# Attention, MoE and routed experts in one kernel: weight loads paced, output weights converted one step later, one chunk's routing moved to TensorE

## The chip, the cores and the metric

One core of a Trainium2 chip runs the whole program. The metric is device microseconds of one execution on that core, lower is better. A measurement of this kernel can tell about 0.2% from no change.

## What is computed

Three stages follow each other, all in float32 for 2304 tokens: windowed attention with 8 heads, a gated product of two projections, and eight experts of which each token uses one.

```python
def _attn_ref(q, k, v):               # q, k, v: (4, 8, 576, 64)
    scores = scale * np.matmul(q, k.transpose(0, 1, 3, 2))
    mask = (rel >= 0) & (rel < 128)
    scores = np.where(mask, scores + bias[None], -1000000000.0)
    scores = scores - np.max(scores, axis=-1, keepdims=True)
    attn = np.exp(scores)
    attn = attn / (np.sum(attn, axis=-1, keepdims=True) + 1e-09)
    return np.matmul(attn, v)

def _moe_ref(x, w_a, w_b, w_out):     # float64 weights, 512 x 1536 and 1536 x 512
    return ((x @ w_a) * (x @ w_b)) @ w_out

def _moe2_ref(x, modality_id, w_gate, modality_bias, w1, w2):
    logits = x @ w_gate + modality_bias[modality_id]
    e_idx = np.argmax(logits, axis=1)
    ...
    for e in range(E):
        h = np.maximum(x[mask] @ w1[e], 0.0)
        out[mask] = gate_w[mask, None] * (h @ w2[e])
```

## The kernel before

The tokens are cut into 18 tiles of 128 and these into seven chunks of 3, 2, 2, 3, 3, 3 and 2 tiles. For each chunk c the program takes 12 steps j, one for each block of 128 columns of the inner width 1536. A step multiplies the chunk by block j of both projections (`mm_ab`, L502: 24 matmuls, since weight and data are each split into a rounded part and a remainder), multiplies the two results (`gf`), and adds the previous step's result times a block of the output weights to the accumulators (`mm_out`, L515 in chunk 0, L519 later). Between these, each step advances the attention of the next chunk's tiles: `score_mm` (L254, L258), select and maximum (L266, L272), exponential (L282), sum and reciprocal (L288, L290), norm (L301), transposes (`pt_tr`, L310), mask selection on GpSimd (L326, L328), product with the values (`a_pv`, L378) and its evacuation (`pv_out`, L387).

The weights arrive as float64. In chunk 0 they are converted as the steps go. For a weight pair (block j of both projections, 1 MB, `wab_load`, L435) VectorE builds float32 words in three operations (`f64_ops`: `one`, L422, and two `more`, L426; the tile is `f64f`), ScalarE casts the rounded part (`hi`, L449) and VectorE subtracts for the remainder (`rest`, L452). `wab_jobs` returns these five jobs in that order. An output weight (512 KB, `wo_load`, L464) needs three operations (`wo_jobs`, tile `f64o`); it is used in that form in chunk 0 and stored (`wo_f`, L475) for the later chunks. The raw and the converted output weights share four buffers. `step00` is step 0 of chunk 0 and `step0` every other step of it.

TensorE, ScalarE and VectorE run in the order in which the program is written; SP's queue, which issues nearly all transfers in order, is ordered by the scheduler. In `step0` the list `da` holds the remainder of pair j + 1 and the three word operations of pair j + 2, the list `db` the two operations on the softmax sums and the three of the output weight, and they are taken in turns.

The routing of a finished chunk (logits, argmax, place in the expert's list) has two forms, chosen by `RD`. A chunk in `RD` gets dot products on VectorE: `rd_step` runs one expert a step, one operation per tile (`junk`, L601), with the expert's gate row broadcast by a 256 KB load (`wgt`, L596). Any other chunk gets `route`: four transposes (L531), a copy, eight small matmuls (L539) and the rank chain (`route_fin`), one tile after another in `step`. Before the change chunk 0 uses `route` and chunks 1 to 5 use dot products; the dot products of chunk c run in the steps of chunk c + 1.

Of the kernel before, what the change touches and what calls it, by code (L numbers as in the profile page):

```python
# [16 lines left out]
P = 128  # L17
# [4 lines left out]
def attn_moe_moe2(ctx: ExitStack, tc, q, k, v, moe_w_a, moe_w_b, moe_w_out, modality_id,  # L22
# [15 lines left out]
    SK = 3  # L38
    CAP = 0
    QD = 1  # L40
    RD = (1, 2, 3, 4, 5)
    PCB = 1
    LDA = 6
    SAT = 3
# [235 lines left out]
    def score_exp(it):  # L280
        for h in range(2):
            nc.scalar.activation(out=it.p[:, h, :], in_=it.p[:, h, :], func=AF.Exp, bias=it.mx[:, 2 + h:3 + h],  # L282
                                 scale=-1.0, accum_out=it.mx[:, 4 + h:5 + h])
# [177 lines left out]

    def wo_load(j):
        r = m1.tile([P, DM, 2], U32, tag="wo", bufs=WOB, name="wor")
        nc.sync.dma_start(out=r.rearrange("p a b -> p (a b)"), in_=moe_w_out.bitcast(U32)[j * P:(j + 1) * P, :])  # L464
        wraw["o", j] = r

    def wo_jobs(j):
# [509 lines left out]
    def step00():  # L977

        n, p1 = CH[0] * P, pairs[1, 0]
        w1, w2, wo = job.pop(1)[3:], wab_jobs(2), wo_jobs(0)  # L980
        job[2] = w2
        i0 = live[n0] = score_mm(p1, 0)
        mm_ab(0, 0, 0, (3,))
        i1 = live[n0 + 1] = score_mm(p1, 1)
        mm_ab(0, 0, 1, (3,))
        w1[0]()
        score_red(i0)
        w1[1]()
        asb = m1.tile([P, MT * P], F32, tag="asb", bufs=1, name="asb")
        nc.scalar.copy(out=asb[:, :n], in_=ab_ps[0][:, :n])  # L990
        gf = m1.tile([P, MT * P], F32, tag="g", bufs=2, name="gf")
        nc.vector.tensor_tensor(out=gf[:, :n], in0=ab_ps[1][:, :n], in1=asb[:, :n], op=ALU.mult)
        score_exp(i0)
        score_inv(i0)
        score_red(i1)
        prep_va(p1)
        score_nrm(i0)
        mm_ab(0, 1, 0)
        wo[0]()
        pt_tr(i0)  # L1000
        pt_cp(i0)
        prep_vd(p1)
        score_exp(i1)
        w2[0]()
        score_inv(i1)
        score_nrm(i1)
        for f in (wo[1], w2[1], wo[2], w2[2], w2[3]):
            f()
        new_preps(goal[2], goal[0])
        cur["s"] = goal[0]  # L1010
        return (0, 0, gf), [n0 + 1], [n0]

    def step0(j, pend, sc, tp):
# [4 lines left out]
        if j + 2 < NJ:  # L1018
            job[j + 2] = wab_jobs(j + 2)
        js = job.get(j + 2, [])  # L1020

        da = [job.pop(j + 1)[4]] if j + 1 in job else []
        da += js[:3]
        di = [f for g in sc for f in score_invs(live[g])]
        dw = wo_jobs(j)
        db = di[:1] + dw[:1] + di[1:] + dw[1:]
        while da or db:
            for d in (da, db) if j > 1 else (db, da):
                if d:
                    d.pop(0)()  # L1030
        psa = mm_ab(0, j, 0) if j > 1 else ab_ps[0]
        asb = m1.tile([P, MT * P], F32, tag="asb", bufs=1, name="asb")
        nc.scalar.copy(out=asb[:, :n], in_=psa[:, :n])
# [14 lines left out]
        for g in new:  # L1048
            c_, hp_, t_ = items[g]
            live[g] = score_mm(pairs[c_, hp_], t_)  # L1050
        for f in js[3:4]:
            f()
        for g in new:
            score_red(live[g])
        for g in new:
            score_exp(live[g])
        new_preps(goal[j + 2], goal[j])
        mm_out(*pend, wo_t[j - 1])
        if last:
# [8 lines left out]
    def step(c, j, pend, sc, tp):  # L1068
# [23 lines left out]
        for r in ranks:  # L1092
            if r[0] < 2:
                next(r[1])
                r[0] += 1
        if c > 2:
            rd_step(j)
        new_preps(goal[k + 2], goal[k])
        if c == 1 and j + 2 < NJ:
            wo_fetch(j + 2, c)  # L1100
# [28 lines left out]
            x_split(c + 1, range(1, KD))  # L1129
        for g in new:  # L1130
            score_exp(live[g])
        if c == 2:
            rd_step(j)
        if pend is not None:
            mm_out(*pend)
        if tr and tr[0][0] in (0, 2, 4):
# [59 lines left out]
    for c in range(NC):  # L1196
        n = CH[c] * P
        for j in range(NJ):
            if c == 0:
                if j == 0:  # L1200
                    pe.enter_context(tc.manual_schedule(engines={
                        mybir.EngineType.PE, mybir.EngineType.Activation, mybir.EngineType.DVE}))
                if j + 4 < NJ:
                    wab_load(j + 4)
                if j + 1 < NJ:
                    wo_load(j + 1)
                if j == CJ:
                    with tc.issue_after(mark["pt"]):
                        consts_b()
# [307 lines left out]
```

## Time and profile before

| what | value |
|---|---|
| median of 3 runs | 838.18 us (838.05 to 838.37) |
| profiled execution | 838.99 us, span 837.2 us |
| mean granted TensorE clock | 0.989 |
| TensorE matmuls busy | 803.4 us (96%) |
| weight loads busy | 721.1 us (86%) |
| VectorE / ScalarE / GpSimd busy | 563.1 / 460.0 / 237.4 us |
| data moved | 147.23 MB, mean 176 GB/s |

Busy shares are averages over stages that differ: a stage's own limit is read from its windows and from what each idle stretch waited for. A row's idle time stands in brackets with the engine and line that released it.

### The profile page before, as it was taken

To read this page: it belongs to the slowest core of one execution; us is meant where nothing else is said; L and a number is where in the kernel's file an instruction comes from. 1 tells how busy PE (TensorE), PEld (TensorE's weight loads), DVE (VectorE), ACT (ScalarE), POOL (GpSimd) and SP (SyncE) were. 2 spreads that over 40 slices of the span, in tenths; PEclk is the share of its full clock that TensorE was granted. 3 is DMA by queue.
4 is the path that set the end of the run, shared out by engine and by line. 5 is a ranking of instruction groups with operands and counts; after the bars stand their busy time and mean duration, and the time that the engine had idled before them with its cause. 6 is when DMAs were issued, how large, how long until landed. Compare 5 with 4: busy or idle time off the path is not lost.

```text
span 837.2 us, 14381 instructions
## 1 busy us (share of the span) xinstructions
PE 803.4 (96%) x4662; PEld 721.1 (86%) x4662; DVE 563.1 (67%) x1603; ACT 460.0 (55%) x1159; POOL 237.4 (28%) x365
## 2 busy tenths in 40 slices
PE   9969999999998999999999999999999999999994
PEld 7856777999887899999999999999888998979893
DVE  7778997777788776667877776468575544447420
ACT  7844555877766766666666644233345443547410
POOL 5312242343344332232222331120133030115101
PEclk9998999999999999999999999999999999999997
DMA  8993336676666795554555544557428554649301
GB/s 240 377 391 104 115 111 191 198 229 218 194 185 191 197 211 161 151 152 136 161 153 155 129 142 123 147 165 241 169 83 306 193 193 134 168 135 303 117 25 40
DMA packets 79781, 147.23 MB, mean 176 GB/s; under 512 B 14223, under 2 KB 42031, under 8 KB 79696
## 3 DMA queue, kind: packets, MB, share of 16 engines
q1 hardware_dynamic: 76144, 136.48, 54.1%
q0 software_dynamic: 3552, 9.73, 3.2%
q8 instruction: 39, 0.64, 0.3%
q14 instruction: 46, 0.38, 0.2%
HBM read 120.25 MB, written 22.12 MB: 170 GB/s over the span
## 4 chain that ended last, share of the span: by engine, by line
PE 63%; DVE 12%; issue 8%; DMA 8%; ACT 5%; POOL 2%; SPq 1%; POOLq 0%; ACTq 0%; DVEq 0%
PE ps_ab L502 26%; PE acc L519 10%; PE ps_h L1270 8%; PE ps_y L1253 7%; PE acc L515 3%; DVE junk L601 3%; PE ps_o L378 2%; DMA wraw<-in_moe_w_b 2%; PE ps_s L258 2%; PE ps_p L310 1%; DMA wraw<-in_moe_w_a 1%; DMA wo_f<-f64o 1%; DMA kk<-in_k 1%; DMA tab<-tinit 1%; DVE p L272 1%
## 5 line engine op out<-in xcount | busy, mean ns | idle before, releaser
L502 PE MATMUL ps_ab<-xr,wab 128*128 128x384 f32 (+1 forms) x2016 | 326.2, 316 | 1.9 <-DVE gf L1167 1.0
L502 PEld LDWEIGHTS ps_ab<-xr,wab 128*128 128x128 f32 x2016 | 307.3, 188 | 14.0 <-issue 4.4
L519 PE MATMUL acc<-wo,g 128*128 128x512 f32 x540 | 135.1, 393 | 0.0
L326 POOL TENSOR_SCALAR_AFFINE_SELECT pt<-pc 128x512 fp32r<-128x512 f32 (+1 forms) x72 | 46.3, 643 | 269.3 <-DVE pc L324 244.2
L519 PEld LDWEIGHTS acc<-wo,g 128*128 128x128 f32 x540 | 96.9, 188 | 16.9
L1270 PE MATMUL ps_h<-xT,w1s 128*128 128x384 f32 x576 | 104.3, 337 | 0.0
L1253 PE MATMUL ps_y<-w2s,h 128*128 128x512 f32 x432 | 104.0, 394 | 0.0
L1270 PEld LDWEIGHTS ps_h<-xT,w1s 128*128 128x128 f32 x576 | 99.7, 188 | 1.3 <-issue 0.5
L1253 PEld LDWEIGHTS ps_y<-w2s,h 128*128 128x128 f32 x432 | 79.8, 188 | 15.7
L601 DVE CUSTOM_DVE_ANT_0 junk<-x,wgt 128x512 f32<-128x512 f32 x104 | 77.4, 744 | 2.9 <-DMA wgt<-in_wgt 0.6
L282 ACT ACTIVATE p<-p,mx 128x128 f32<-128x128 f32 x144 | 56.8, 396 | 31.0 <-DVE mx L272 30.7
L301 ACT ACTIVATE p<-p,mx 128x128 f32<-128x128 f32 x120 | 41.7, 395 | 38.8 <-DVE mx L290 38.6
L387 ACT COPY u<-ps_o 64x384 f32<-64x384 f32 x120 | 56.9, 474 | 7.6 <-PE ps_o L378 6.2
L1105 ACT CAST g<-gf 128x384 fp32r<-128x384 f32 (+1 forms) x60 | 28.2, 470 | 50.6 <-DVE gf L1103 50.2
L1106 DVE TENSOR_TENSOR g<-gf,g 128x384 fp32r<-128x384 f32 (+1 forms) x60 | 30.3, 505 | 37.8 <-ACT g L1105 37.3
L886 DVE TENSOR_TENSOR w2s<-wr,w2s 128x1024 fp32r<-128x1024 f32 x24 | 29.4, 1225 | 38.0 <-ACT w2s L885 37.9
L1260 POOL DMA_INDIRECT out<-y,idx x18 | 21.2, 1176 | 114.7 <-ACT y L1259 113.2
L1103 DVE TENSOR_TENSOR gf<-ps_ab,asb 128x384 f32<-128x384 f32 (+1 forms) x60 | 30.1, 502 | 29.6 <-PE ps_ab L502 22.6
L1273 ACT ACTIVATE h<-ps_h 128x384 fp32r<-128x384 f32 x48 | 23.6, 492 | 44.0 <-PE ps_h L1270 44.0
L886 DVE TENSOR_TENSOR w1s<-wr,w1s 128x1024 fp32r<-128x1024 f32 x28 | 34.3, 1224 | 16.7 <-ACT w1s L885 16.7
L392 POOL TENSOR_TENSOR xf<-u 128x128 f32<-128x128 f32 x60 | 33.9, 564 | 39.5 <-ACT u L387 39.5
L328 POOL TENSOR_SCALAR_AFFINE_SELECT pt<-pc 128x512 fp32r<-128x512 f32 (+1 forms) x72 | 45.0, 625 | 0.0
(218 smaller groups left out, 1207.5 us busy)
## 6 DMA issues: line engine op xcount, KB each, us to landing
wo<-wo_d SPq DMA_DIRECT2D x60, 512.0 KB, 4.2
wr<-in_moe_w SPq DMA_DIRECT2D x56, 512.0 KB, 4.8
wgt<-in_wgt SPq DMA_DIRECT2D x40, 256.0 KB, 3.6
wraw<-in_moe_w_a SPq DMA_DIRECT2D x12, 512.0 KB, 8.9
wraw<-in_moe_w_b SPq DMA_DIRECT2D x12, 512.0 KB, 8.6
wor<-in_moe_w_out SPq DMA_DIRECT2D x12, 512.0 KB, 3.9
wo_d<-wo SPq DMA_DIRECT2D x12, 512.0 KB, 3.1
kr<-in_k SPq DMA_DIRECT2D x24, 256.0 KB, 4.3
```

Of the source, the lines that this page charges most:

```text
L282: nc.scalar.activation(out=it.p[:, h, :], in_=it.p[:, h, :], func=AF.Exp, bias=it.mx[:, 2 + h:3 + h], scale=-1.0, accum_out=it.mx[:, 4 + h ...
L301: nc.scalar.activation(out=it.p[:, h, :], in_=it.p[:, h, :], func=AF.Copy, scale=it.mx[:, 6 + h:7 + h])
L326: nc.gpsimd.affine_select(out=it.pt[:, :, 0], in_=pc, pattern=pat + [[-1, P]], base=0, channel_multiplier=1, compare_op=ALU.is_gt, fill=0.0)
L328: mark["pt"] = nc.gpsimd.affine_select(out=it.pt[:, :, 1], in_=pc, pattern=pat + [[1, P]], base=0, channel_multiplier=-1, compare_op=ALU.i ...
L387: nc.scalar.copy(out=u[o:o + 64], in_=it.po[o:o + 64, 1 - h:4 - h])
L392: nc.gpsimd.tensor_tensor(out=xf, in0=u[:, 0], in1=u[:, 2], op=ALU.add)
L502: nc.tensor.matmul(ps[:, :n], lhsT=w[:, m, r, kk * P:(kk + 1) * P], rhs=xr[:, s, kk, :n], start=(idx == 0), stop=(idx == len(terms) - 1))
L519: nc.tensor.matmul(acc[c, t], lhsT=g[:, r, t * P:(t + 1) * P], rhs=w[:, s, :], start=(j == 0 and idx == 0), stop=(j == NJ - 1 and idx == 2))
L601: nc.vector.tensor_tensor_reduce(out=junk, in0=x2[:, 0:DM], in1=wgt[0][:, e % 2], scale=1.0, scalar=0.0, op0=ALU.mult, op1=ALU.add, accum_ ...
L886: nc.vector.tensor_tensor(out=dst[:, 1], in0=srcw, in1=dst[:, 0], op=ALU.subtract)
L1253: nc.tensor.matmul(pss[t], lhsT=h[:, r, f, t * P:(t + 1) * P], rhs=W2[f // 2][:, s_, f % 2, :], start=(f == 0 and i == 0), stop=(f == 7 an ...
L1270: nc.tensor.matmul(ps, lhsT=W1[f // 2][:, r, kk, (f % 2) * P:(f % 2 + 1) * P], rhs=xT[:, s_, kk, :], start=(kk == 0 and i == 0), stop=(kk ...
```

## The change

In chunk 0, from step 2 on, the output weight converted in step j is j - 1 (the last step does two), and it is loaded one step later. From step 1 to step 7 the load of weight pair j + 4 is put behind the latest output weight load in SP's queue. The turns of the two lists are written out, with the sums' and the output weight's operations ahead of the next pair's words. In step 0 the cast of pair 2 is left out and done in step 1 behind the new tile's score product; step 1's other weight work comes after its exponential. Chunk 1 leaves `RD`, so its routing is done by `route` in chunk 2.

```diff
-    RD = (1, 2, 3, 4, 5)
+    RD = (2, 3, 4, 5)
...
     def wo_load(j):
         r = m1.tile([P, DM, 2], U32, tag="wo", bufs=WOB, name="wor")
-        nc.sync.dma_start(out=r.rearrange("p a b -> p (a b)"), in_=moe_w_out.bitcast(U32)[j * P:(j + 1) * P, :])
+        mark["wo"] = nc.sync.dma_start(out=r.rearrange("p a b -> p (a b)"),
+                                       in_=moe_w_out.bitcast(U32)[j * P:(j + 1) * P, :]).ins
...
-        for f in (wo[1], w2[1], wo[2], w2[2], w2[3]):
+        for f in (wo[1], w2[1], wo[2], w2[2]):
             f()
...
-        da = [job.pop(j + 1)[4]] if j + 1 in job else []
+        w = job.pop(j + 1, None)
+
+        di = [f for g in sc for f in score_invs(live[g])]
+        dw = [f for i in ((j - 1, j) if last else (j - 1,)) if j > 1 for f in wo_jobs(i)]
+        da, db = [w[4]] if w else [], di[:1] + dw[:1] + di[1:] + dw[1:]
         da += js[:3]
-        di = [f for g in sc for f in score_invs(live[g])]
-        dw = wo_jobs(j)
-        db = di[:1] + dw[:1] + di[1:] + dw[1:]
-        while da or db:
-            for d in (da, db) if j > 1 else (db, da):
-                if d:
-                    d.pop(0)()
+        for d in () if j == 1 else (da, db, db, db, da, db, da, db, da, db, db, db):
+            if d:
+                d.pop(0)()
+        assert j == 1 or not da and not db
...
-        for f in js[3:4]:
-            f()
+        if j == 1:
+            w[3]()
+        else:
+            for f in js[3:4]:
+                f()
         for g in new:
             score_red(live[g])
         for g in new:
             score_exp(live[g])
+        if j == 1:
+            for f in da + js[3:4]:
+                f()
...
-        if c > 2:
-            rd_step(j)
+        rd_step(j)
...
-        if c == 2:
-            rd_step(j)
...
-                if j + 4 < NJ:
-                    wab_load(j + 4)
-                if j + 1 < NJ:
-                    wo_load(j + 1)
+                if j == 0:
+                    wab_load(4)
+                if j != 1:
+                    wo_load(max(j, 1))
+                if 0 < j < NJ - 4:
+                    with tc.issue_after(mark["wo"]):
+                        wab_load(j + 4)
```

Three places show how the instructions move. The first is chunk 0, steps 0 to 2. On ScalarE the cast of pair 2 (`wab_765`, now `wab_815`) stood between the norm of step 0 (L301) and the scaling of the next query pair (L232):

```order
 L282 ACTIVATE p,mx<-p,mx 128x128 x2
 L301 ACTIVATE p<-p,mx 128x128 x2
-L449 CAST wab_765<-f64f 128x2x512
 L232 ACTIVATE qq<-qr_1_671,qscale 64x256 x2
-L1033 COPY asb<-ps_ab_727 128x384
-L323 CAST pc<-ps_p 128x2x128
-L387 COPY u<-ps_o 64x384 x2
+L1034 COPY asb<-ps_ab_727 128x384
+L323 CAST pc<-ps_p 128x2x128
+L387 COPY u<-ps_o 64x384 x2
+L449 CAST wab_815<-f64f 128x2x512
```

It now follows the evacuation of step 1 (L387). On VectorE, in step 2, pair 3's remainder (`wab_829`), the sums (L288, L290), output weight 2 (`f64o`) and pair 4's words (`wraw_666`) stood like this:

```order
L452 TENSOR_TENSOR wab_829<-f64f,wab_829 128x2x512
L288 TENSOR_SCALAR mx<-mx 128x2
L422 TENSOR_SCALAR f64f<-wraw_666 128x1024
L422 TENSOR_SCALAR f64o<-wor 128x512
L426 SCALAR_TENSOR_TENSOR f64f<-wraw_666,f64f 128x1024
L290 RECIPROCAL mx<-mx 128x2
L426 SCALAR_TENSOR_TENSOR f64f<-wraw_666,f64f 128x1024
L426 SCALAR_TENSOR_TENSOR f64o<-wor,f64o 128x512 x2
```

And now, with pair 2's remainder (`wab_815`) and pair 3's words (`wraw_209`) just ahead, at the end of step 1, and output weight 1 in the place of 2:

```order
L452 TENSOR_TENSOR wab_815<-f64f,wab_815 128x2x512
L422 TENSOR_SCALAR f64f<-wraw_209 128x1024
L426 SCALAR_TENSOR_TENSOR f64f<-wraw_209,f64f 128x1024 x2
L452 TENSOR_TENSOR wab_829<-f64f,wab_829 128x2x512
L288 TENSOR_SCALAR mx<-mx 128x2
L422 TENSOR_SCALAR f64o<-wor 128x512
L290 RECIPROCAL mx<-mx 128x2
L422 TENSOR_SCALAR f64f<-wraw_666 128x1024
L426 SCALAR_TENSOR_TENSOR f64o<-wor,f64o 128x512
L426 SCALAR_TENSOR_TENSOR f64f<-wraw_666,f64f 128x1024
L426 SCALAR_TENSOR_TENSOR f64o<-wor,f64o 128x512
L426 SCALAR_TENSOR_TENSOR f64f<-wraw_666,f64f 128x1024
```

The reciprocal has moved ahead of pair 4's words, and the output weight's last operation ahead of the pair's.

The second place is SP's queue ahead of the values of the next head pair (`vr_1_673`). Before, the weight pairs stood there in a row up to the last; `wraw_1102` to `wraw_1272` are pairs 9 to 11, `wraw_846` and `wraw_945` pairs 6 and 7:

```order
L435 DMA wraw_1102<-in_moe_w_b 128x1024
L435 DMA wraw_1184<-in_moe_w_a 128x1024
L435 DMA wraw_1184<-in_moe_w_b 128x1024
L435 DMA wraw_1272<-in_moe_w_a 128x1024
L435 DMA wraw_1272<-in_moe_w_b 128x1024
L435 DMA wraw_846<-in_moe_w_a 128x1024
L435 DMA wraw_846<-in_moe_w_b 128x1024
L435 DMA wraw_945<-in_moe_w_a 128x1024
L435 DMA wraw_945<-in_moe_w_b 128x1024
L156 DMA qr_2_675<-in_q 128x256
L464 DMA wor<-in_moe_w_out 128x1024
L161 DMA vr_1_673<-in_v 128x3x128
```

Now, with `wraw_841` pair 6 and `wraw_940` pair 7:

```order
L464 DMA wor<-in_moe_w_out 128x1024
L435 DMA wraw_841<-in_moe_w_a 128x1024
L435 DMA wraw_841<-in_moe_w_b 128x1024
L161 DMA vr_1_673<-in_v 128x3x128
L156 DMA qr_3_679<-in_q 128x256
L476 DMA wo_f<-f64o 128x512
L390 DMA z<-u 64x128 x2
L464 DMA wor<-in_moe_w_out 128x1024
L435 DMA wraw_940<-in_moe_w_a 128x1024
L435 DMA wraw_940<-in_moe_w_b 128x1024
```

Of the pairs that stood ahead of the values only 5 and 6 are left there; pair 7 and the later ones each follow an output weight load. The store of output weight 0 (`wo_f`) is the one of its kind that comes first, before and now.

The third place is VectorE in chunk 2, between the maximum (L272) and the sums (L288) of one tile. Before, the two dot products (L601) stood there in each of eight steps:

```order
L272 ISA mx 128x1
L601 ISA junk,lgr<-x_2779,wgt 128x512
L601 ISA lgr 128x1
L601 ISA junk,lgr<-x_2782,wgt 128x512
L601 ISA lgr 128x1
L288 TENSOR_SCALAR mx<-mx 128x2
```

Now no L601 is left in this chunk. In two steps for each of the two tiles stand rows of the rank chain, here those of the second of these steps:

```order
L272 ISA mx 128x1
L559 TENSOR_SCALAR sc<-sc 128x1
L560 RECIPROCAL x_2776<-sc 128x1
L577 TENSOR_TENSOR osum<-osum,oh 128x8
L579 TENSOR_TENSOR ra<-ps_r,ereg 128x8
L580 TENSOR_TENSOR ra<-ra,oh 128x8
L581 TENSOR_REDUCE sc<-ra 128x1
L582 CAST po_all<-sc 128x1
L288 TENSOR_SCALAR mx<-mx 128x2
```

TensorE gets, once for each tile, four transposes (L532), eight small products (L540) and the two matmuls that give the rank (L575, L576).

## Rows read from the trace of the kernel before

**Rows 1.** Stage windows: us, busy us (count) of PE, PEld, DVE, ACT, POOL, PEclk.

```profile
36.70:71.03 34.33, 25.15 (x98) 18.75 (x98) 28.60 (x58) 15.99 (x44) 6.85 (x13) 0.85 0.86 321
...
78.47:134.08 55.61, 55.20 (x260) 43.91 (x259) 53.76 (x97) 26.79 (x64) 20.36 (x27) 1.00 0.44 130
...
144.09:212.50 68.41, 67.89 (x501) 62.98 (x499) 49.80 (x172) 55.04 (x154) 25.96 (x41) 1.00 0.68 214
212.50:289.80 77.30, 70.69 (x479) 62.27 (x479) 60.74 (x194) 52.72 (x152) 31.82 (x48) 1.00 0.66 183
```

**Rows 2.** Timeline of PE, 26 to 90 us: start, us, what, idle before.

```profile
50.74 2.07 PE L254 MATMUL ps_s<-kk,qq 128*128 128x256 f32 x4 [4.07 <-ACT qq L232]
...
64.63 0.76 PE L310 MATMUL ps_p<-ident,p 128*128 128x128 f32 x2 [4.08 <-ACT p L301]
...
66.89 4.70 PE L515 MATMUL acc<-f64o,gf 128*128 128x512 f32 x6
71.03 4.73 PE L502 MATMUL ps_ab<-xr,wab 128*128 128x384 f32 x24
...
76.29 2.74 PE L515 MATMUL acc<-f64o,gf 128*128 128x512 f32 x6
```

**Rows 3.** Windows after the second stop, and in chunk 2.

```profile
64.00:66.00 2.00, 1.37 (x4) 1.13 (x5) 1.97 (x5) 1.21 (x4) 0.00 (x0) 0.50 0.01 2
...
251.00:255.00 4.00, 2.94 (x17) 2.35 (x17) 3.36 (x11) 3.11 (x8) 0.72 (x2) 1.00 0.69 213
```

**Rows 4.** Timeline of ACT, 26 to 90 us.

```profile
49.23 1.04 ACT L449 CAST wab<-f64f 128x1024 fp32r<-128x1024 f32 x1 [3.03 <-DVE f64f L426]
...
61.68 0.51 ACT L197 CAST vv<-vr 128x384 fp32r<-128x384 f32 x1 [3.30 <-DMA vr<-in_v]
```

**Rows 5.** Timelines of DVE, 26 to 90 and 88 to 165 us.

```profile
62.45 0.43 DVE L422 TENSOR_SCALAR f64o<-wor 128x512 uint32<-128x512 uint32 x1 [2.54 <-DMA wo_f<-f64o]
...
86.39 1.22 DVE L452 TENSOR_TENSOR wab<-f64f,wab 128x1024 fp32r<-128x1024 f32 x1
...
92.78 0.55 DVE L1039 TENSOR_TENSOR gf<-ps_ab,asb 128x384 f32<-128x384 f32 x1
...
94.46 1.58 DVE L452 TENSOR_TENSOR wab<-f64f,wab 128x1024 fp32r<-128x1024 f32 x1
```

**Rows 6.** Timeline of SP's queue, 14 to 75 us.

```profile
39.05 0.33 SPq L435 DMA_DIRECT2D wraw<-in_moe_w_a  x1
...
53.05 0.38 SPq L161 DMA_DIRECT2D vr<-in_v  x1
```

**Rows 7.** Waits, 212.5 to 289.8 us: us, times, longest.

```profile
ACT p L301 <- DVE mx L290: 15.1, 11, 1.8
```

**Rows 8.** Lines of DVE by form, 212.5 to 289.8 us.

```profile
L601 DVE CUSTOM_DVE_ANT_0 junk<-x,wgt 128x512 f32<-128x512 f32 x16 | 15.0, 939 | 0.3
```

**Rows 9.** Tile f64f, 36 to 140 us: ns min/median/max, starts.

```profile
L426 DVE SCALAR_TENSOR_TENSOR f64f<-wraw,f64f x20: 1212/1220/1479, 46.3 to 122.4; 128x1024 uint32<-128x1024 uint32 x20
L452 DVE TENSOR_TENSOR wab<-f64f,wab x11: 1216/1490/2341, 39.2 to 126.6; 128x1024 fp32r<-128x1024 f32 x11
L422 DVE TENSOR_SCALAR f64f<-wraw x10: 682/694/949, 44.0 to 120.2; 128x1024 uint32<-128x1024 uint32 x10
```

**Rows 10.** Tile f64o, 36 to 140 us.

```profile
L426 DVE SCALAR_TENSOR_TENSOR f64o<-wor,f64o x24: 678/686/1017, 45.3 to 135.1; 128x512 uint32<-128x512 uint32 x24
```

**Rows 11.** Timeline of PE, 186 to 300 us: chunk 2's step starts.

```profile
216.78 2.98 PE L502 MATMUL ps_ab<-xr,wab 128*128 128x256 f32 x24
...
222.25 3.01 PE L502 MATMUL ps_ab<-xr,wab 128*128 128x256 f32 x24
...
281.00 1.57 PE L502 MATMUL ps_ab<-xr,wab 128*128 128x256 f32 x12
```

**Rows 12.** Chain of waits, chunk 1: start us, us, what; weight products.

```profile
155.24 2.95 PE ps_ab L502 x24
...
172.94 2.95 PE ps_ab L502 x24
```

## The prediction

> **What bounds the kernel now.** I read four views in this order. The windows by stage come first [rows 1]: TensorE is busy all the time in chunk 0 from 78 us on (55.20 of 55.61 us) and nearly so in chunk 1, but it stands for 9.2 of the 34.3 us from 36.7 to 71.0 and for 6.6 of the 77.3 us of chunk 2. These two stages are the ones that the change touches; a microsecond won there stays won, since the rest waits on TensorE.
>
> TensorE's timeline then shows what the first stage loses [rows 2]. There are two stops of about 4.1 us, at 46.7 and at 60.5. After the second the granted clock is at the lower of its two levels (0.50 of full speed, so 1.2 GHz, [rows 3]): the output product of step 2 takes 4.14 us from start to start (66.89 to 71.03) where step 3's takes 2.18 (76.29 to 78.47, where step 4 and the second window of [rows 1] begin).
>
> ScalarE and VectorE tell why [rows 4, 5]. The first stop is the scaling of the next query pair: it stands in ScalarE's queue behind the cast of weight pair 2, which starts at 49.23 after 3.03 us idle, until VectorE has rebuilt that pair's words. The second has two late transfers in it: ScalarE waits 3.30 us for `vr` (to 61.68), VectorE 2.54 us for the store of output weight 0, whose buffer output weight 2 is to take (to 62.45); the softmax norm before the transposes at 64.63 needs both engines. On SP's queue `vr` is issued at 53.05 only, behind the weight pairs [rows 6], and that store next.
>
> In chunk 2 the waits say: ScalarE's norm waits 15.1 us, 11 times, for VectorE [rows 7]. Just ahead of the reciprocals that it needs stand two routing dot products a step, 16 of 939 ns in all [rows 8].
>
> **The change, part by part.** Times are those of the profiled execution (838.99 us, span 837.2); the runs' median, 838.18, lies 0.8 below, and I carry the difference over to it.
>
> *First stop.* Without the cast in front, the scaling can begin when ScalarE falls idle, 49.23 - 3.03 = 46.2. Before, TensorE started 0.5 us after the cast's end (49.23 + 1.04 = 50.27), so it goes on at 46.7 instead of 50.74: the stop is gone. The output product needs the words of output weight 0. In VectorE's queue they are followed by the last operation on pair 2 (1.2 us, [rows 9]), which ends at 49.2; so they are there at 48.0, and the product ends at 48.0 + 2.18 = 50.2.
>
> *What is late next.* Pair 2's cast comes at 49.2 to 50.2. Its remainder (L452) now stands behind one product, one pc and one tile's select and max. The same sequence took 94.46 - 92.78 = 1.68 us in step 5 [rows 5], so it starts at 50.9 and, taking the 1.58 us of that place, ends at 52.5. Two of step 2's 24 weight products can run ahead of it. TensorE therefore waits from 50.6 to 52.5, **a new wait of 1.9 us**, and its 22 other products (4.2 us) and the attention product end at 57.1.
>
> *Second stop.* VectorE rebuilds pair 3 in 52.5 to 55.6 (0.7 + 2 x 1.2, [rows 9]), ScalarE casts for 1.0, the remainder for 1.2 us, to 57.8. Ahead of the norm there then stand only three small operations, the sums' two and the first on output weight 1. Before, 64.63 - 62.45 = 2.2 us passed from such a first operation to the transposes, with one of 1.2 us for pair 4 in between; without it 1.0, and 0.1 for the sum. The transposes start at 58.9, 5.7 us before 64.63, after **a second new wait of 1.8 us**. That needs the transfers to be early: `vr` now stands five issues behind pair 5, where 39.05 was [rows 6]; with the 8.6 us that it took before (53.05 to 61.68) it lands at 47.7, 9 us before use. Output weight 1, converted in this step now, takes the buffer of raw weight 0, which no store holds; the store of output weight 0, two issues behind `vr`, is wanted a step later.
>
> *Step 2's output product* now needs output weight 1, converted in this very step: after the reciprocal (58.3, half a microsecond ahead of the transposes) come 0.7 + 0.7 + 1.2 + 0.7 = 3.3 us at most, 3.1 as starts overlap a little [rows 9, 10]. It runs 61.4 to 63.6 at the full clock: step 3 starts 7.4 us before 71.03.
>
> *Step 3* gives some back. VectorE at 61.4 still has 1.2 for pair 4, 0.5 for the values, the 1.68, the remainder 1.58, the three small ones 0.5 and again 3.1: 69.9. TensorE wants output weight 2 at 63.6 + 5.26 (71.03 to 76.29) = 68.9. After this wait of 1.0 step 4 starts at 72.1 instead of 78.47, 6.4 us earlier. From there VectorE needs 8.07 us a step (86.39 to 94.46, [rows 5]) and TensorE 55.61 / 7 = 7.94; step 4 has no norm to wait for, so VectorE regains a lead; over six steps the 0.13 more may cost a few tenths, and I take **6.2 us** for chunk 0. Moving one output weight's 1.7 us out of each step to the next costs nothing: the last two are done in step 11, where no pair is left. Bounds: VectorE was idle 7.5 us from 36.7 to 78.5 (5.7 of it before 71.0, [rows 1]) and 1.7 us of work moves behind, so at most 9.2; if the clock falls after the new waits, 6.2 - 3.0 = 3.2 (2.0 for the output product, 1.0 for what lies around it).
>
> *SP's queue.* A weight pair's two loads now follow the raw output weights, whose buffer VectorE must have read. For pair 7 this is at 61.4 and its words are wanted in step 5, some 20 us later; the others keep that distance of two steps and a half. It is hidden; rival 4 is what happens if not.
>
> *Chunk 1's routing.* The 16 dot products go, and eight 256 KB weight broadcasts. From 222.25 to 281.00 TensorE takes nine steps of 6.53 us; the step before, ahead of the first dot product, took 5.47 [rows 11]. Nine times the difference is 9.5 us. The price: each of two tiles gets transposes, eight small products, a copy and its rank chain, which chunk 1 already does for chunk 0's tiles. Three steps there, with one full round of it, took 17.70 us [rows 12] against 3 x 5.47 = 16.4, and one of the three had no score product (0.5): 1.8 a tile, 3.5 for two. Sum 6.0.
>
> The measure of the stall matters here. By TensorE's idle time the stage can return only 6.6, so 6.6 - 3.5 = 3.1; by step length 6.0. I take the second: the steps' starts count all of the time, idle time only what no record covers. The Trainium skill (Perfetto Trace Analysis, Identifying the Most-Contended Engine) says that matmul busy time misleads and that the busy share of weight loads is to be read instead. By that rule, with weight loads at 62.98 / 68.41 = 92% in chunk 1 and 62.27 / 77.30 = 81% in chunk 2, the same loads at 92% would take 67.7 us, 9.6 less; this agrees with the steps' 9.5. Upper bound 9.5 - 2 x 1.2 = 7.1, with the small products alone.
>
> **Sum:** 6.2 + 6.0 = 12.2 us. Median 838.18 - 12.2 = **826.0**.
>
> **Rivals.**
> 1. *The clock falls again.* The second stop of 4.1 us was followed by the lower level; a gap of 1.1 us in 251 to 255 was not [rows 3]. No row shows what 1.9 us does; two of them come close together. It is nearer to the short one, so I expect 2.4 GHz. If not: 838.18 - 3.2 - 6.0 = 829.0. For it: TensorE works only 4.6 us between the two.
> 2. *Chunk 2's chain without dots is longer than TensorE's step*, through ScalarE's scaling and casts: then only the idle time comes back, 838.18 - 6.2 - 3.1 = 828.9. Against it: chunk 1 runs that chain with twelve weight splits besides, and loses 0.5 us.
> 3. *VectorE can't follow in chunk 0.* Its 8.07 is above TensorE's 7.94, and the remainder, 1.22 alone, went up to 2.34 [rows 9]. At 0.5 us more a step for six steps 3.0 is lost: 829.0. The Trainium skill (SBUF — State Buffer, Who interferes with whom) gives the cause: an operation with two SBUF inputs is locked out while GpSimd reads. By that rule the remainders now placed right behind the mask selections pay each time; the 1.58 us used above agrees.
> 4. *Slower: the weight pairs come late.* If SP hangs on a buffer and each of pairs 6 to 11 reaches VectorE d us late, 6 x d is paid: at d = 3 the time is 826.0 + 18 = 844. It decides from d = 12.2 / 6 = 2.0; with the margin above, a load would need over 20 us where `vr`, in the fullest queue, needed 8.6.
> 5. *The change doesn't do what it says:* SP's order leaves `vr` or that store late. Then the second stop stays, and 838.18 - 4.0 - 6.0 = 828.2.
>
> **How the numbers follow.** Forecast 0.55; rivals 0.14, 0.14, 0.10, 0.04 and 0.03. The range goes from both upper bounds (9.2 + 7.1: 821.9) to both lower ones (3.2 + 3.1: 831.9), which takes in rivals 1, 2, 3 and 5: 822 to 832. A measurement tells some 0.2% (1.7 us) from no change. Faster by more: all but rival 4 and a pile-up of the others, 0.94; within: 0.02; slower: 0.04.
>
> **What would show it.** Right: TensorE idle before the first score product of step 1 gone; two or three waits of 1 to 2 us before step 4, released by L452, by the norm and by output weights; step 4 some 6 us earlier; clock 1.00 throughout; nine steps of chunk 2 in about 53 us; no wgt load before chunk 3. Wrong: a granted clock of 0.50 between 50 and 65 us, VectorE idle on a transfer after 60 us, or chunk 2's norm still waiting 10 us for VectorE.

## The result and the profile after

| | before | after |
|---|---|---|
| median (of 4 runs each) | 838.12 us (835.88 to 838.37) | 825.68 us (824.82 to 826.96) |
| ratio | 1 | 0.9859, 95% interval 0.9836 to 0.9881 |
| profiled execution | 838.99 us | 824.82 us |
| forecast | | 826.0 us (822 to 832) |

The change takes 12.4 us off by the medians (11.8 by the ratio), against 12.2 forecast. The sum came out; how it divides did not, as the sections below show. First the page of the changed kernel, part 1 (busy us, share of the span, instructions): TensorE is busy for 798.7 us (803.4 before), its share of the span is up by one point to 97%, and VectorE has lost 16 us of work.

```profile
span 823.0 us, 14381 instructions
...
PE 798.7 (97%) x4686; PEld 720.5 (88%) x4686; DVE 547.0 (66%) x1571; ACT 460.4 (56%) x1161; POOL 235.0 (29%) x365
```

The stage windows of the changed kernel, cut where those of [rows 1] were (up to the start of step 3 of chunk 0, chunk 0 from step 4 on, chunk 1, chunk 2):

```profile
36.70:64.34 27.64, 23.03 (x98) 16.55 (x98) 24.35 (x54) 13.96 (x38) 7.08 (x12) 0.94 0.60 222
...
71.89:127.43 55.54, 54.85 (x260) 43.91 (x259) 53.75 (x97) 26.47 (x64) 23.64 (x28) 1.00 0.63 204
...
137.44:205.28 67.84, 67.60 (x501) 62.98 (x499) 49.25 (x171) 54.41 (x153) 25.38 (x40) 1.00 0.70 215
205.28:275.50 70.22, 69.16 (x507) 64.15 (x505) 47.56 (x168) 54.39 (x157) 27.36 (x50) 1.00 0.63 174
```

TensorE was idle for 9.2 us ahead of step 3; now it is 27.64 - 23.03 = 4.6. In chunk 2 the idle 6.6 us have become 1.1, and weight loads are busy for 64.15 of 70.22 us, or 91%, where it was 81%. The parts in between are as long as before (55.54 us for 55.61, 67.84 for 68.41).

TensorE's timeline, chunk 0, around the two former stops:

```profile
46.38 1.23 PE L254 MATMUL ps_s<-kk,qq 128*128 128x256 f32 x4
47.85 2.84 PE L516 MATMUL acc<-f64o,gf 128*128 128x512 f32 x6 [0.24 <-DVE f64o L426]
...
52.16 4.08 PE L503 MATMUL ps_ab<-xr,wab 128*128 128x384 f32 x22 [1.11 <-DVE wab L452]
...
58.73 0.62 PE L310 MATMUL ps_p<-ident,p 128*128 128x128 f32 x2 [2.01 <-ACT p L301]
...
61.16 3.75 PE L516 MATMUL acc<-f64o,gf 128*128 128x512 f32 x6 [0.47 <-DVE f64o L426]
64.34 4.73 PE L503 MATMUL ps_ab<-xr,wab 128*128 128x384 f32 x24
...
69.61 2.84 PE L516 MATMUL acc<-f64o,gf 128*128 128x512 f32 x6
71.89 4.74 PE L503 MATMUL ps_ab<-xr,wab 128*128 128x384 f32 x24
```

The first stop is gone: step 1's score product follows at 46.38 with no wait, where 50.74 with 4.07 us stood [rows 2]. Weight pair 2's remainder (L452) is waited for at 52.16, for 1.11 us, and the norm at 58.73, for 2.01. The transposes come 5.9 us earlier than before, step 4 comes 6.6 earlier. One thing is not as it was forecast: the output product at 61.16 takes 3.18 us to the next row, where step 3's takes 2.28 (69.61 to 71.89). Windows of one microsecond show why (the number before the last two is the granted clock):

```profile
60.00:61.00 1.00, 0.68 (x2) 0.00 (x0) 1.00 (x2) 0.65 (x2) 0.19 (x1) 0.50 0.00 0
...
62.00:63.00 1.00, 1.00 (x2) 0.34 (x1) 1.00 (x3) 0.73 (x1) 1.00 (x1) 0.50 0.70 240
63.00:64.00 1.00, 1.00 (x4) 0.50 (x3) 0.96 (x4) 0.32 (x1) 0.44 (x2) 0.99 0.18 63
```

After the wait at 56.7 to 58.7 TensorE runs at 0.50 of full speed, the lower of its two levels, for 3.4 us: from 59.6 (the window 59 to 60 has a mean of 0.80) to 63.0.

In chunk 2 the step starts are these:

```profile
210.14 0.60 PE L532 MATMUL ps_x<-ident,x 128*128 128x128 f32 x4
210.49 3.10 PE L503 MATMUL ps_ab<-xr,wab 128*128 128x256 f32 x24
...
215.64 0.95 PE L540 MATMUL ps_l<-wg,x2T 128*128 128x8 f32 x8
216.45 3.07 PE L503 MATMUL ps_ab<-xr,wab 128*128 128x256 f32 x24
...
251.55 2.98 PE L503 MATMUL ps_ab<-xr,wab 128*128 128x256 f32 x24
...
267.64 2.98 PE L503 MATMUL ps_ab<-xr,wab 128*128 128x256 f32 x24
```

A step without any part of the routing takes 5.36 us (16.09 for the three from 251.55 to 267.64). The nine steps from 216.45 to 267.64 take 51.19 us instead of 58.75 [rows 11]. The two rows ahead of 210.49 and of 216.45 are the transposes and the small products of `route` for the first tile. The waits of the chunk (205.28 to 274.4 us) show the norm, 15.1 us before [rows 7]:

```profile
ACT p L301 <- DVE mx L290: 6.3, 11, 0.9
```

### The profile page after: what moved, and what is told of

Same layout as the page of the kernel before. It is cut to its first block, busy times and chain, and to the rows that moved or that the text cites. A ratio compares the mean times of both kernels' runs of the same rounds, so it can differ in the third digit from the quotient of the medians.

```text
span 823.0 us, 14381 instructions
## 1 busy us (share of the span) xinstructions
PE 798.7 (97%) x4686; PEld 720.5 (88%) x4686; DVE 547.0 (66%) x1571; ACT 460.4 (56%) x1161; POOL 235.0 (29%) x365
## 4 chain that ended last, share of the span: by engine, by line
PE 64%; DVE 11%; issue 9%; ACT 8%; DMA 4%; POOL 2%; SPq 0%; POOLq 0%; ACTq 0%
PE ps_ab L503 28%; PE acc L520 11%; PE ps_h L1277 7%; PE ps_y L1260 6%; PE acc L516 3%; PE ps_o L378 3%; PE ps_s L258 2%; ACT p L282 2%; PE ps_p L310 2%; DVE f64f L426 1%; DMA idx<-tab 1%; DVE junk L602 1%; DMA wr<-in_moe_w 1%; PE ps_s L254 1%; DVE w1s L887 1%
## 5 line engine op out<-in xcount | busy, mean ns | idle before, releaser
L602 DVE CUSTOM_DVE_ANT_0 junk<-x,wgt 128x512 f32<-128x512 f32 x88 | 62.0, 704 | 2.7 <-DMA wgt<-in_wgt 0.7
L387 ACT COPY u<-ps_o 64x384 f32<-64x384 f32 x120 | 56.8, 473 | 7.6 <-PE ps_o L378 6.2
L301 ACT ACTIVATE p<-p,mx 128x128 f32<-128x128 f32 x120 | 41.7, 395 | 26.4 <-DVE mx L290 26.2
L328 POOL TENSOR_SCALAR_AFFINE_SELECT pt<-pc 128x512 fp32r<-128x512 f32 (+1 forms) x72 | 45.2, 628 | 0.0
L1281 DVE SCALAR_TENSOR_TENSOR h<-ps_h,h 128x384 fp32r<-128x384 f32 x48 | 26.3, 554 | 27.4 <-ACT h L1280 27.1
```

The source lines that it names most:

```text
L328: mark["pt"] = nc.gpsimd.affine_select(out=it.pt[:, :, 1], in_=pc, pattern=pat + [[1, P]], base=0, channel_multiplier=-1, compare_op=ALU.i ...
L387: nc.scalar.copy(out=u[o:o + 64], in_=it.po[o:o + 64, 1 - h:4 - h])
L602: nc.vector.tensor_tensor_reduce(out=junk, in0=x2[:, 0:DM], in1=wgt[0][:, e % 2], scale=1.0, scalar=0.0, op0=ALU.mult, op1=ALU.add, accum_ ...
```

## The experiments

The runs were made in four sets, each on one chip with runs of the kernel before among them; ratios are to those.

### Each half alone

The first kernel is the one before with one line of the diff:

```diff
-    RD = (1, 2, 3, 4, 5)
+    RD = (2, 3, 4, 5)
```

> The kernel before with chunk 1's routing on TensorE as the only edit. In the two profiles chunk 2 (from its first weight product to chunk 3's step 1) is 7.9 us shorter after the change. Theory, the parts stand side by side: 838.1 - 7.9 = 830.2 us (829.3 to 831.2), and the steps of chunk 2 without any routing take 5.36 us as after the change. By the prediction's own term it would be 832.1. Rival, the gain in chunk 2 hangs on the new order of chunk 0 as well (what SP still has to move when chunk 2 starts): over 834.

Measured: 829.51 us, ratio 0.9898 (0.9872 to 0.9923), so 8.5 us faster, as the theory has it. Chunk 2 gives what it gives in the full change: from its first weight product at 209.76 to the third step of chunk 3 (j = 2) at 292.19 it takes 82.4 us, as after the change (205.28 to 287.64), against 90.2 before (211.90 to 302.12). It needs nothing of chunk 0.

The second is the changed kernel without that line, the dot products in their old place:

> The changed kernel with chunk 1's routing put back on VectorE (dot products at their old place), so that only the edits in chunk 0 are left. Theory: step 4 of chunk 0 starts near 71.9 us and stays 6.4 to 6.6 us ahead of the kernel before to the end: 831.7 us (830.8 to 832.5), and chunk 2's steps are 6.5 us again. Rival, part of the lead of chunk 0 is lost in chunk 1 or 2 to a wait that was hidden: over 833.

Measured: 833.57 us, ratio 0.9948 (0.9931 to 0.9964), 4.4 us faster. The time is past the 833 of the rival, but not for its reason: in the trace the lead is not lost in chunk 1 or 2, it is smaller from step 4 on (4.2 us there, 4.8 at the third step of chunk 3, 297.30 against 302.12). Up to 59 us the trace reads like that of the changed kernel; then:

```profile
59.07 0.62 PE L310 MATMUL ps_p<-ident,p 128*128 128x128 f32 x2 [2.01 <-ACT p L301]
...
61.50 5.49 PE L516 MATMUL acc<-f64o,gf 128*128 128x512 f32 x6 [0.94 <-DVE f64o L426]
66.00 5.58 PE L503 MATMUL ps_ab<-xr,wab 128*128 128x384 f32 x24
...
74.28 4.72 PE L503 MATMUL ps_ab<-xr,wab 128*128 128x384 f32 x24
```

```profile
66.00:67.00 1.00, 1.00 (x3) 0.48 (x2) 1.00 (x5) 0.35 (x1) 0.55 (x1) 0.50 0.00 0
67.00:68.00 1.00, 1.00 (x5) 1.00 (x5) 1.00 (x2) 0.00 (x0) 0.00 (x0) 0.68 0.45 129
```

The clock falls at 60.8 us and stays at 0.50 up to 67.6, for 6.8 us instead of 3.4. The output product takes 4.5 us instead of 3.18, and step 3's weight products 5.58 us instead of 4.73. Step 4 starts at 74.28, only 4.2 us ahead of the kernel before. At the ends of the two traces (spans of 834.3 and 837.2 us) 2.9 are left; the rest goes behind that step, where no edit is. This execution, at 836.14 us, is the longest of the six (the shortest took 831.87), so how much of the 2 us the median lost in this way is not shown. The two halves together, 8.5 + 4.4, make 12.9 us; the full change has 11.8 (10.0 to 13.7) by its ratio. They add up.

### Is the length of the lower clock a property of the program?

> The changed kernel once more, unedited, beside the others of this chip. Its first profile had 3 us at the lower clock after the wait for the norm (60 to 63 us), the run with chunk 0's edits alone had 6 us of it and came 2.4 us later to step 4, with the same program up to there. Theory: the length of that fall differs between executions, and the times of one kernel with it; this run gives 825.7 us (824.5 to 827), with step 4 anywhere between 71.9 and 74.5 us. Rival: it belongs to the program, and step 4 starts at 71.9 within 0.3 again.

Measured: 826.0 us, ratio 0.9861 (0.9843 to 0.9879). In this execution of the same program step 4 starts at 72.87, not 71.89, so the rival is out.

```profile
61.00:62.00 1.00, 0.52 (x1) 0.50 (x2) 1.00 (x2) 0.00 (x0) 0.98 (x2) 0.74 0.16 33
...
64.00:65.00 1.00, 1.00 (x3) 0.35 (x2) 0.97 (x6) 0.47 (x3) 1.00 (x2) 0.55 0.65 188
```

```profile
72.87 4.73 PE L503 MATMUL ps_ab<-xr,wab 128*128 128x384 f32 x24
```

The theory holds in part only: the fall is as long as in the first trace, 3.4 us, but it begins at 61.5 us instead of 59.6, with the output product, and ends at 64.9. Three other kernels have the same engine instructions up to that place and the same wait of 2.0 us. The one of the section on chunk 2 (`e6_dots_early`) shows 3.4 us (58.7 to 62.2) and step 4 at 71.98; the half above and the one with later pairs (`e10_pairs_later`) show 6.8 us (60.8 to 67.6, 60.6 to 67.4) and step 4 at 74.28 and 74.15. The first stop of the kernel before does the same: behind 4.07 us the fall takes 3.4 us in its profile (50.3 to 53.8) and 6.8 us in that of the first experiment (49.9 to 56.7), which has the same chunk 0. So both lengths come behind the same instructions, while no two profiles of one and the same program differ in the length.

The runs without a profile have only their mean granted clock. For the kernel before it goes from 0.987 to 0.992 among the 15 runs on one chip, which is some 8 us more or less at the lower level (an estimate: 0.005 x 837 / 0.5). In the five runs of this kernel here the time goes with it (826.98 us at 0.991, 824.73 at 0.994), in those of the kernel before it does not (836.92 us at 0.987, 839.47 at 0.992). So one profile is worth 2 us either way here, and the 6.6 us of the first one is the better end of what chunk 0 gives.

### The parts of chunk 0's change

The kernel before with nothing but the paced loads:

```diff
-                if j + 4 < NJ:
-                    wab_load(j + 4)
+                if j == 0:
+                    wab_load(4)
                 if j + 1 < NJ:
                     wo_load(j + 1)
+                if 0 < j < NJ - 4:
+                    with tc.issue_after(mark["wo"]):
+                        wab_load(j + 4)
```

> The kernel before with the weight pairs' loads paced behind the output weights' as the only edit; conversions, their order and the cast of pair 2 stay. The first stop (46.7 to 50.7 us) stays. Theory, the second stop is made by the late values and the late store: both come some 5 us earlier, the transposes start near 61.5 instead of 64.63 and TensorE's clock does not fall there, so 3 to 6 us are won: 832 to 835 us. Rival, VectorE's queue is the limit at that place and the transfers only fill its idle time: the transposes come within 1 us of where they were and the time is over 836.5.

Measured: 835.72 us, ratio 0.9972 (0.9961 to 0.9984), 2.3 us faster, between the two expectations.

```profile
50.78 2.07 PE L254 MATMUL ps_s<-kk,qq 128*128 128x256 f32 x4 [4.07 <-ACT qq L232]
...
62.04 0.62 PE L310 MATMUL ps_p<-ident,p 128*128 128x128 f32 x2 [1.24 <-ACT p L301]
...
73.34 4.73 PE L503 MATMUL ps_ab<-xr,wab 128*128 128x384 f32 x24
```

The first stop stays, with its 4.07 us. The transposes move to 62.04 and their wait falls from 4.08 to 1.24 us, as the theory has it, and the clock holds there. The trace is 5.1 us ahead at step 4, yet the median moved by 2.3 only. A second trace with the old chunk 0, that of the first experiment, shows why:

```profile
64.04 0.62 PE L310 MATMUL ps_p<-ident,p 128*128 128x128 f32 x2 [2.13 <-ACT p L301]
...
75.34 4.73 PE L502 MATMUL ps_ab<-xr,wab 128*128 128x384 f32 x24
```

There the wait is 2.13 us without any pacing, the clock is at 1.00 from 57 to 76 us, and step 4 starts 3.1 us earlier than in the profile before. Against this trace pacing is worth 2.0 us at the transposes and at step 4, like the median; that the clock holds can't be put down to it.

The changed kernel with the cast of pair 2 back in step 0:

```diff
-        for f in (wo[1], w2[1], wo[2], w2[2]):
+        for f in (wo[1], w2[1], wo[2], w2[2], w2[3]):
...
-        if j == 1:
-            w[3]()
-        else:
+        if j > 1:
```

> The changed kernel with the cast of weight pair 2 back in step 0, ahead of the scaling of the next query pair. Theory: the first stop of about 4 us before step 1's score product returns, with the lower clock after it; in exchange the wait for pair 2's remainder (1.1 us) goes and that for the norm (2.0) shrinks, so 2 to 4 us are lost: 827.7 to 829.7 us. Rival, VectorE's conversions pace chunk 0 up to step 4 whatever TensorE does: step 4 starts within 0.8 us of 71.9 and the time is 825.7 within 0.8.

Measured: 828.15 us, ratio 0.989 (0.9863 to 0.9916), as expected. By the ratios (0.9861 for the changed kernel) the cast's old place costs 2.4 us; its four runs (827.20 to 829.26) all lie above the nine of the changed kernel (824.73 to 826.98), on other chips.

```profile
50.50 2.08 PE L254 MATMUL ps_s<-kk,qq 128*128 128x256 f32 x4 [4.07 <-ACT qq L232]
...
61.66 0.48 PE L310 MATMUL ps_p<-ident,p 128*128 128x128 f32 x2
...
74.69 4.72 PE L503 MATMUL ps_ab<-xr,wab 128*128 128x384 f32 x24
```

The stop is back (4.07 us for L232), the lower clock follows it (49.7 to 56.5 us), and the waits for pair 2's remainder and for the norm are gone: the row at 61.66 has no wait.

The changed kernel with the pairs issued as before:

```diff
-                if j == 0:
-                    wab_load(4)
+                if j + 4 < NJ:
+                    wab_load(j + 4)
                 if j != 1:
                     wo_load(max(j, 1))
-                if 0 < j < NJ - 4:
-                    with tc.issue_after(mark["wo"]):
-                        wab_load(j + 4)
```

> The changed kernel with the weight pairs' loads issued as before, not behind an output weight's, so that the values of the next head pair stand behind eleven weight pairs again. Theory: the values land near 61 us, ScalarE's norm waits for them, the transposes of step 2 start near 62.5 instead of 58.7 and 3 to 5 us are lost: 828.5 to 830.5 us. Rival, with one output weight less to convert and the cast moved the place has slack of its own: under 826.7.

Measured: 828.44 us, ratio 0.9892 (0.9876 to 0.9909): 2.4 us are lost of the changed kernel's 826.0 on the same chip.

```profile
61.10 0.51 ACT L197 CAST vv<-vr 128x384 fp32r<-128x384 f32 x1 [4.64 <-DMA vr<-in_v]
```

```profile
62.47 0.76 PE L310 MATMUL ps_p<-ident,p 128*128 128x128 f32 x2 [5.73 <-ACT p L301]
...
67.88 4.73 PE L503 MATMUL ps_ab<-xr,wab 128*128 128x384 f32 x24
```

ScalarE waits 4.64 us for the values, TensorE 5.73 us for the norm. This is the prediction's fifth rival, brought about by the edit; it was priced at 828.2.

The loads paced harder still, each of the pairs from 5 on one step later:

```diff
-                if 0 < j < NJ - 4:
+                if 1 < j < NJ - 3:
                     with tc.issue_after(mark["wo"]):
-                        wab_load(j + 4)
+                        wab_load(j + 3)
```

> The changed kernel with the weight pairs 5 to 11 each loaded one step later. It measures the margin of the loads that now wait behind output weights. Theory: a pair is issued 20 to 30 us before its words are built, a step is 8 us, so nothing waits: 825.7 us within 0.8. Rival, the margin is under a step: VectorE idles on raw pairs, each of five or more pairs some us late: over 828.

Measured: 827.92 us, ratio 0.988 (0.9857 to 0.9903), above the theory's band and below the rival's bound. No wait of VectorE for a raw weight is in the trace; it has the long fall of the clock (60.6 to 67.4 us), and its step 4 at 74.15 is 2.2 us behind that of the changed kernel's first trace, as much as the median is. So the loads have a margin of a step at least, and whether the later loads have to do with the long fall is open.

### VectorE as the limit of chunk 0

The waits that are left in steps 2 and 3 can be moved. In step 2 VectorE idles 1.11 us ahead of pair 3's remainder, and output weight 1 could be done there:

```diff
-        for d in () if j == 1 else (da, db, db, db, da, db, da, db, da, db, db, db):
+        for d in () if j == 1 else (da,) * (j > 2) + (db,) * 8 + (da,) * 4:
```

> The changed kernel with another order on VectorE: in step 2 the sums and all of output weight 1 stand ahead of pair 3's remainder, in later steps all of the output weight ahead of the next pair's words. Theory: the 1.1 us that VectorE idles before pair 3's remainder are filled, the norm comes about 0.9 us earlier, the wait of step 2's output product goes, and TensorE's clock falls less or not at all: 1 to 3 us won, 822.7 to 824.7 us. Rival, VectorE is the limit from 52 to 70 us and what is taken earlier is lost in step 3 or 4: 825.7 within 0.8. Second rival, pair 4's words come too late for ScalarE's cast: over 827.

Measured: 827.17 us, ratio 0.9878 (0.986 to 0.9896): no gain, 1.2 us worse than the changed kernel on the same chip if anything. In the trace step 3 starts at 61.2 us, 3.1 earlier, the clock stays at 1.00 throughout, step 4 starts at 69.85. Then every step is late and step 11 starts at 129.36, 1.9 us after that of the changed kernel. With the remainder of pair 2 ahead of the tile's select and maximum as well (in step 1 `da.pop(0)()` right after `w[3]()`):

> The same with pair 2's remainder taken ahead of the tile's select and maximum in step 1. Theory: TensorE's wait for that remainder (1.1 us in the changed kernel) falls to about 0.5, and 0.3 to 0.8 us more are won than with the other order alone. Rival, the select and maximum come later by as much and the exponential with them, so nothing is won beside it, or up to 0.5 us lost.

Measured: 827.46 us, ratio 0.9879 (0.9861 to 0.9896). TensorE's wait for the remainder falls from 1.12 to 0.52 us, that for the norm grows from 0.99 to 1.75, and nothing is won. With the new order in steps 2 and 3 only (`j < 4`) and the order of the change behind them:

> The changed kernel with the output weight ahead only in steps 2 and 3 of chunk 0, later steps in the order of the change. Theory: steps 2 and 3 are won as with that order everywhere (step 4 near 69.9 us, no lower clock at 60 us), and from there VectorE, with 54.3 us of work in 56, gives back most but not all of the 2 us: 824 to 825.5 us. Rival, VectorE has no reserve and all is given back by step 11: 825.7 to 827.

Measured: 825.48 us, ratio 0.9858 (0.9839 to 0.9877), the same as the changed kernel.

```profile
57.82 0.62 PE L310 MATMUL ps_p<-ident,p 128*128 128x128 f32 x2 [1.00 <-ACT p L301]
...
69.96 4.73 PE L503 MATMUL ps_ab<-xr,wab 128*128 128x384 f32 x24
...
87.47 4.74 PE L503 MATMUL ps_ab<-xr,wab 128*128 128x384 f32 x24
...
127.24 4.74 PE L503 MATMUL ps_ab<-xr,wab 128*128 128x384 f32 x24
```

Step 4 is 1.9 us ahead of the changed kernel's first trace, step 6 has 0.3 of that left and step 11 0.2. To see who takes it back, VectorE was given less to do. The third operation on each output weight but the first is left out, the one that fills in the three lowest bits of the mantissa, so the weights are not quite the same:

```diff
+        if short:
+            return [one, lambda: (more(1, 0xC0000000, ALU.bitwise_and), done())]
...
-        return f64_ops(wraw.pop(("o", j)), f, done)
+        return f64_ops(wraw.pop(("o", j)), f, done, j > 0)
```

> The kernel with the output weight ahead in steps 2 and 3, less one of the three VectorE operations on each output weight but the first (the one that fills in the three lowest bits of the mantissa is left out, 0.69 us a step, 7.5 us over chunk 0; it says nothing of a kernel that computes the same). Theory: from step 4 of chunk 0 on VectorE is the limit, and this is why the 2 us won in steps 2 and 3 were gone by step 6. With less work for VectorE step 4 starts at 69.5 us or earlier, the lead of 8 us over the kernel before is there still at the end of chunk 0, and the time is 823 to 824.5 us. Rival, TensorE's 7.9 us a step take the lead back for another reason (the exponential's chain or GpSimd's selection): the lead falls to 6.8 again and the time is 825.5 within 0.7.

Measured: 821.59 us, ratio 0.9811 (0.9798 to 0.9825), even below the theory's band.

```profile
68.79 4.73 PE L505 MATMUL ps_ab<-xr,wab 128*128 128x384 f32 x24
...
123.43 4.73 PE L505 MATMUL ps_ab<-xr,wab 128*128 128x384 f32 x24
```

The stretch from 72 to 126 us of the two kernels, this one second:

```profile
72.00:126.00 54.00, 52.73 (x247) 41.32 (x246) 53.31 (x94) 25.20 (x58) 23.11 (x27) 1.00 0.57 189
```

```profile
72.00:126.00 54.00, 54.00 (x256) 43.17 (x255) 50.05 (x93) 26.59 (x63) 20.65 (x26) 1.00 0.64 201
```

With 3.3 us less of work on VectorE in that stretch TensorE never stops (54.00 of 54.00 us, 52.73 above), and step 11 starts 10.7 us ahead of the kernel before instead of 6.8. So it is VectorE's work that took the lead back. In the changed kernel itself the two engines are near a balance from step 4 on: TensorE is busy for 54.85 of 55.54 us, VectorE for 53.75.

### Chunk 2: the dot products or their place

The changed kernel with chunk 1 back in `RD`, but the dot products where the later chunks have them:

> The changed kernel with chunk 1's routing on VectorE again, but its dot products at the place that the later chunks use, ahead of the product of the two projections, instead of between the maximum and the sums. Theory, it is their place: with the 939 ns operations between maximum and sums the norm and so the transposes are late, and where they stand now the product and the masks are late instead, so the work itself has to go: chunk 2's steps stay above 6.2 us and the time is 832 to 834 us, as with chunk 0's edits alone. Rival, only the place was wrong and VectorE has room for them (47.6 us of other work in 70): steps near 5.5 us, 826 to 828 us.

Measured: 830.35 us, ratio 0.9905 (0.9882 to 0.9929), between theory and rival. By the traces chunk 2, from its first weight product to the third step of chunk 3, takes 90.2 us with the old place (207.12 to 297.30), 86.3 with this one (205.01 to 291.32) and 82.4 without the dot products. Half of the gain was to be had by the place alone, the other half needs the work gone. The ratios (0.9948, 0.9905 and 0.9861) say the same: 3.6 and 3.7 us. The view of the tile `junk` (ns min/median/max) of the kernel before, and of this one:

```profile
L601 DVE CUSTOM_DVE_ANT_0 junk<-x,wgt x18: 679/829/1055, 223.4 to 299.2; 128x512 f32<-128x512 f32 x18
```

```profile
L602 DVE CUSTOM_DVE_ANT_0 junk<-x,wgt x20: 675/692/696, 213.0 to 295.0; 128x512 f32<-128x512 f32 x20
```

The same operation takes 1050 or 830 ns in the old place and 692 in the new. VectorE's and GpSimd's timelines of the kernel before show the neighbour; GpSimd's of this kernel stands third:

```profile
223.41 1.05 DVE L601 CUSTOM_DVE_ANT_0 junk<-x,wgt 128x512 f32<-128x512 f32 x1
```

```profile
223.28 0.63 POOL L328 TENSOR_SCALAR_AFFINE_SELECT pt<-pc 128x512 fp32r<-128x512 f32 x1
223.89 0.89 POOL L393 TENSOR_TENSOR xf<-xf,z 128x128 f32<-128x128 f32 x1
```

```profile
228.48 0.64 POOL L326 TENSOR_SCALAR_AFFINE_SELECT pt<-pc 128x512 fp32r<-128x512 f32 x1 [4.67 <-DVE pc L324]
...
229.68 0.45 POOL L393 TENSOR_TENSOR xf<-xf,z 128x128 f32<-128x128 f32 x1
```

In the old place the dot products ran beside the mask selection (L328) and the addition (L393), and that addition took 0.89 us. In the new one, here at 225.40 and 226.13, GpSimd is idle from 223.8 to 228.5 (4.67 us), and the same addition, at 229.68, takes 0.45.

## Why the prediction held, point by point

- **First stop: right.** It is gone, the score product runs at 46.38 (46.7 forecast) and the output product ends at 50.13 (50.2). Put back, it costs 2.4 us.
- **What is late next: right, smaller.** The wait for pair 2's remainder was put at 1.9 us (50.6 to 52.5) and was 1.11 (51.05 to 52.16).
- **Second stop: right.** Transposes at 58.73 (58.9 forecast) after a wait of 2.01 us (1.8); the output product starts at 61.16 (61.4). The values were issued at 43.88, not 39.05, and are used at 56.34 without a wait. In the old issue order they come at 61.10.
- **The clock after the new waits: wrong.** The step that failed is "It is nearer to the short one, so I expect 2.4 GHz". The sign that the prediction had named for this, a granted clock of 0.50 between 50 and 65 us, is there in all five traces with these instructions, behind the 2.0 us wait. Where that wait was 1.0 us (57.82, with the output weight ahead), or 1.75 with pair 2's remainder ahead as well, the clock held. The length of the wait alone does not tell: in the old chunk 0 the clock held behind 2.13 us (64.04, first experiment). By step 4, forecast at 72.1, the traces have 71.9 to 72.9 with the fall of 3.4 us, and 74.2 and 74.3 with that of 6.8. The short one took about the 1.0 us that the forecast had put down for a wait in step 3 (which did not come, as TensorE was late itself), the long one some 2 us more. So the first rival came true in part.
- **Chunk 0's sum: too high.** 6.2 us were forecast; the half alone measures 4.4 (3.0 to 5.8). Besides the clock, the profile that the terms were read from was late in chunk 0: step 4 at 78.47, where another execution of the same instructions had 75.34. Differences taken from its rows can be up to 3 us too large; how the missing 1.8 us divide between the two was not separated.
- **VectorE, the third rival: the limit, though not the loss that was priced.** The forecast had 8.07 against 7.94 us a step. The lead over the kernel before neither grows nor falls from step 4 (6.6 us) to step 11 (6.7), but a lead of 8.5 at step 4 (69.96) is 6.8 at the end. The upper bound of 9.2 us was not to be had with this work.
- **Chunk 2: too low.** 6.0 us were forecast and 7.9 came by the traces (8.5 by the first experiment). Two terms were mis-sized. The step without routing takes 5.36 us, not the 5.47 of the one step in [rows 11]: 9 x 0.11 = 1.0. And the price of 3.5 us for two tiles was about right (the six steps from 210.49 to 246.20 take 35.71 us, 3.55 over 6 x 5.36), but the rank chain in it was not new. With dot products TensorE's rank products stood at 282.41 and 291.35, in the last step of chunk 2 and step 0 of chunk 3. These two steps take 1.1 us less now (6.71 and 5.90 for 7.12 and 6.63), which I put down to it; no run shows it alone. With 0.3 us more in step 0 (5.21 for 4.88) the sum is 6.0 + 1.0 + 1.1 - 0.3 = 7.8.
- **Steps against idle time: right.** The steps' lengths gave 9.5 us before the price, idle time 6.6. The 7.9 us that came, after the price, are more than all of the idle time. The Trainium skill's rule on weight loads (Perfetto Trace Analysis, Identifying the Most-Contended Engine) gave 9.6, at a share of 92%; the share is 91% now.
- **Slower by late pairs, the fourth rival: no.** VectorE waits for no raw weight, not even with the loads a step later.

The errors of the two halves, some 1.8 us each, have opposite signs. The sum was right to 0.4 us because they cancel, which is luck.

## What to carry to other kernels

When a wait goes, ask of each engine how much of the lead it can use: 2 us won in steps 2 and 3 were worth nothing, since VectorE had no room behind them, and its busy share of the stage ahead (53.3 of 54 us) says so. When work moves to another engine, look for the part of it that the old form has too, or it is paid twice. Where the clock moves, take a term from more than one execution: five with the same instructions differed by 2.4 us at the same step, of which 0.3 was there before the fall.

## What the runs showed of the hardware

The fall of the clock behind one and the same wait of 2.0 us took 3.4 us in three traces and 6.8 us in two, and began 0 to 2.4 us after the wait. This alone spreads chunk 0 by some 2 us. Two executions of one program had the fall 1.9 us apart. A wait of 2.13 us at the same transposes, in the kernel with the old chunk 0, was followed by none.

A VectorE operation with two inputs in SBUF took 692 ns beside an idle GpSimd and up to 1055 ns beside GpSimd's selection and addition, and the addition went from 0.45 to 0.89 us. The Trainium skill (SBUF — State Buffer, Who interferes with whom) says that such an operation contends with a GpSimd instruction that reads SBUF, and the traces agree. For the 16 dot products this is an estimated 16 x 0.25 = 4.0 us of VectorE's time (939 ns on average in [rows 8], 692 here). Whether the gain by their place comes from this or from the norm, which no longer stands behind them, was not separated.
